# A build-time instruction order planned with other durations and a list of kept rank changes

## The chip, the cores and the metric

The kernel runs on one core of one Trainium2 chip. The metric is the device time of one execution in microseconds (us), lower is better. A program is compared with the one before it on the same chip, and the times shown are single executions and their median.

## The reference

Attention over 4 batches, 8 heads, 768 positions and 64 values for each head; three of the heads see every earlier position, five see only four sink positions and a window of 64. The 3072 x 512 result goes through a two-branch layer. In short:

```
scores = q @ k.T / 8;   scores[mask == 0] = -1e9
x = softmax(scores) @ v                          # per batch and head, joined to 3072 x 512
h1, h2 = x @ w1, x @ w2                          # 512 -> 1024
out = maximum(h1, h2) @ w_out                    # 1024 -> 512
```

## The kernel before

The heads are taken in pairs, four pairs to a batch: one pair of two full heads (FF), one of a full and a windowed head (FS), two of windowed heads (SS). So there are 16 pairs, called n0 to n15; n0 to n3 are batch 0, n4 to n7 batch 1, and so on. For a pair the work runs through these operations, whose function names are used below:

- `load_qk`, `load_v`: DMAs issued by SyncE (SP), all in one queue, in the order of the code; `cast_qk` and `cast_v` make bf16 of them, mostly on GpSimd (POOL).
- `turn` and `unturn` transpose q and k through TensorE (PE) for n0 to n7; `turn_squares` does it on VectorE (DVE) for n8 to n15.
- `mix_k` writes `kx`, the keys in the order that windowed heads want, with two copies, on DVE or POOL; `mix_v` writes `vx` on POOL.
- `scores` (PE, line 480) writes one PSUM tile `ps`; `exp` (ScalarE, ACT, line 497) makes `at` of it; `mask` (DVE, line 519) multiplies a 0/1 table into it, for n4 to n15 only (n0 to n3 have a bias matmul, line 453).
- `weighted` (PE, line 541) multiplies `at` with v, once for each score tile and each half of the positions; `normalise` (DVE, lines 556 and 558: one reciprocal, two products) divides and writes x.

When a batch has its x: `turn_x` (PE, line 574) and `take_x` transpose it, for each half; `up` (PE, line 590) multiplies with w1 - w2, eight column blocks fc0 to fc7 for each half tg0 and tg1; `relu` (ACT or DVE) evicts them to `g`; `down` (PE, line 617) makes one block of 128 rows, i0 to i5, in three parts of four matmuls (maximum(h1, h2) is relu(h1 - h2) + h2, so a product of w2 and w_out, `product`, line 690, is prepared and added); `take_out` evicts it and `store` writes it out. `subtract` (line 721, DVE or POOL) makes w1 - w2, `cast_w2` bf16 of w2, `turn_w2` its transpose.

All these are recorded as operations with a cost in microseconds for each engine that may do them. The class `Order` then plans them at build time: `Order.run` steps through modelled time, gives each engine the ready operation of lowest `rank` (the pair's number for most), takes PE's work from seven lists in the priority TX (turn_x), W (weighted), S (scores), TQ (turn), F (up, down), P (product), D (filler), picks one of four PSUM banks for each PE output, and emits the operations in the order found. On the chip each engine runs its instructions strictly in that order and waits by semaphores. So a cost never enters the program as time; it only decides which engine gets an operation and in which order each engine's instructions stand. A helper, `copy`, records most copies and casts, so they all have line 314 (ACT) or 316 (DVE and POOL).

Of the kernel before, what the change touches and what calls it, by code (L numbers as in the profile page):

```python
# [2 lines left out]

# [12 lines left out]
ACT = mybir.ActivationFunctionType  # L16
# [52 lines left out]
WARM = 60  # L69


class Op:


# [9 lines left out]
class Order:  # L84
# [5 lines left out]

    def __init__(self, banks):
        self.ops, self.lists, self.banks = [], {}, banks
        self.users, self.bank, self.queue = [None] * banks, None, None
        self.warm = 0.0

    def op(self, engine, cost, emit, deps=(), **more):
        o = Op(engine, cost, emit, deps, **more)
# [17 lines left out]
        o.behind, self.queue = self.queue, o  # L115
        return o

    def run(self, names, together=(), spare=(), until=0.0, begin=None):
        free = dict.fromkeys(("PE", "SP", "DMA", "ACT", "DVE", "POOL"), 0.0)
        free.update(begin or {})  # L120
        waiting, pending = [], []
        at = {n: 0 for n in names}
        for k, o in enumerate(self.ops):
            o.number = k
            o.left = sum(d.end is None for d in o.deps) + (o.behind is not None)
            for d in o.deps:
                d.users.append(o)
            if o.behind is not None:
                o.behind.followers.append(o)

        def arm(o, t):
            o.ready = max([t] + [d.end + d.tail for d in o.deps])
            if o.engine != "PE":
                heapq.heappush(waiting, (o.ready, o.number, o))

        def release(users, t):
            for u in users:
                u.left -= 1
                if u.left == 0:
                    arm(u, t)  # L140

        def finish(o, end):
            o.end = end
            release(o.users, 0.0)

        def free_bank():

            able = [
                (0.0 if u is None else u.end + u.tail, k)
                for k, u in enumerate(self.users) if u is None or u.end is not None  # L150
            ]
            return min(able) if able else None

        def when(o):

            if o.left:
                return None
            if o.bank:
                found = free_bank()
                return None if found is None else max(o.ready, found[0])  # L160
            return o.ready

        def pick():

            soon = None
            for n in names:
                mine = self.lists.get(n, ())[at[n]:at[n] + 2]
                w = when(mine[0]) if mine else None
                if w is None:
                    continue  # L170
                if n in spare and (t > until or soon and soon[1] < t + mine[0].cost["PE"]):
                    continue
                if n in together and len(mine) > 1 and not mine[0].single:
                    w2 = when(mine[1])
                    if w2 is not None and w2 < w + 2.0:
                        w = max(w, w2)
                if w <= t:
                    return n, w
                if soon is None or w < soon[1]:
                    soon = n, w  # L180
            return soon

        t = 0.0
        for o in self.ops:
            if not o.left:
                arm(o, 0.0)
        while True:
            while waiting and waiting[0][0] <= t:
                pending.append(heapq.heappop(waiting)[2])
            times = [waiting[0][0]] if waiting else []  # L190
            done = False
            for e in ("ACT", "DVE", "POOL", "SP"):
                able = [o for o in pending if e in o.cost or (o.engine == "DMA" and o.by == e)]
                if not able:
                    continue
                if free[e] > t:
                    times.append(free[e])
                    continue
                for o in sorted(able, key=lambda o: (o.rank, o.ready, o.number)):
                    if o.engine == "DMA":  # L200
                        free[e] = t + o.issue
                        start = max(free[e], free["DMA"])
                        free["DMA"] = start + o.cost["DMA"]
                        end = free["DMA"] + 1.6
                    else:
                        end = t + o.cost[e]
                        if any(max(free[x], t) + c < end for x, c in o.cost.items() if x != e):
                            continue
                        free[e] = end
                    pending.remove(o)  # L210
                    o.emit(e)
                    release(o.followers, t)
                    finish(o, end)
                    done = True
                    break
            if free["PE"] <= t:
                best = pick()
                if best and best[1] <= t:
                    n = best[0]
                    now = t  # L220
                    for k in range(2 if n in together and not self.lists[n][at[n]].single else 1):
                        mine = self.lists[n][at[n]:at[n] + 1]
                        w = when(mine[0]) if mine else None
                        if w is None or w > now + 0.3:
                            break
                        o = mine[0]
                        at[n] += 1
                        if o.bank:
                            self.bank = free_bank()[1]
                            self.users[self.bank] = o.bank  # L230
                        o.emit("PE")
                        now += o.cost["PE"] * (2 if now < self.warm else 1)
                        finish(o, now)
                    free["PE"] = now
                    done = True
                elif best:
                    times.append(best[1])
            else:
                times.append(free["PE"])
            if done:  # L240
                continue
            later = [x for x in times if x > t]
            if not later:
                break
            t = min(later)
        for n in spare:
            for o in self.lists.get(n, ())[at[n]:]:
                o.end = t
        left = sum(o.end is None for o in self.ops)
        assert not left, f"{left} operations were not reached"  # L250
        return t


def tile_paired_heads(tc, q, k, v, w1, w2, w2f, wo, out, tab, heads):
# [490 lines left out]
    def prepare_w12(half, rank):  # L745
        for two in range(2):
            if half:
                loaded = load(1.6, load_w2(half, two))
                prepare_w2(half, two, loaded, rank)
            else:  # L750
                loaded = w2_left[two]
            old, frees = take("qn")
            o = load(1.6, load_w1(half, two), old)
            for c in range(2):
                subs[half, two, c] = op(
                    None, {"DVE": 0.68, "POOL": 1.45}, subtract(half, two, c), [o, loaded], rank=rank
                )
                frees.append(subs[half, two, c])

# [4 lines left out]
    def prepare_qk(n):  # L764
# [22 lines left out]
            bfrees.append(un)  # L787
            ready.append(un)
        if "S" in SLOTS[n % HP]:
            cost = {"DVE": 0.8 if n < HP else 0.5, "POOL": 1.1}  # L790
            ready.append(op(None, cost, mix_k(n), [*ready], rank=n))
        k_ready[n] = ready

    def prepare_v(n):
        old, frees = take("vn")
        mine = [load(1.05, load_v(n, hh), [*old, sorted_], issue=0.5) for hh in range(2)]
        done_with["v", n] = take("v")
        cast = op("POOL", 0.88, cast_v(n), [*mine, *done_with["v", n][0]], rank=n)
        frees.append(cast)
        v_ready[n] = [cast]  # L800
        if "S" in SLOTS[n % HP]:
            cost = 0.5 if SLOTS[n % HP] == "FS" else 0.75
            v_ready[n] += [op("POOL", cost, mix_v(n, lower), [cast], rank=n) for lower in (True, False)]

    frees_ps = []
# [1 line left out]
    def attend(n):  # L807
        biased = n < HP
        for t in tiles_of[n]:
# [3 lines left out]
            if biased:  # L813
# [5 lines left out]
            e = op("ACT", 0.2 + sum(w) / 1240, exp(n, t), [s, *old], rank=n)  # L819
            frees_ps.append(e)  # L820
            mask_ops[n, t] = [e] if biased else [
                op("DVE", 0.13 + part[1] * part[2] / 1700, mask(n, t, *part), [e], rank=n)
                for part in mask_products(n, t)
            ] or [e]
            done_with["qk", n][1].append(s)
# [1 line left out]
        for half in range(2):  # L827
            mine = [t for t in tiles_of[n] if used(n, t, half)]
            if (p, half) == (0, 0):
                done_with["x", b] = take("x")  # L830
            norm = op("DVE", 1.0, normalise(n, half), [*done_with["x", b][0]], rank=n)
            for t in mine:
                w = pe(
                    "W", len(used(n, t, half)) * 0.031 + 0.03,
# [87 lines left out]
    for _ in range(WARM):  # L922
        pe("D", 0.43, warm, bank=order.given(0.0))

    order.warm = 8.4
    order.run(
        ("TX", "W", "S", "TQ", "F", "P", "D"), together=("S",), spare=("D",), until=20.0,
        begin={"DMA": 5.8, "SP": 4.6, "DVE": 5.4, "ACT": 4.8, "POOL": 5.0, "PE": 4.7},
# [536 lines left out]
```

## Time and profile before

| what | value |
| --- | --- |
| median of 3 runs | 190.68 us (189.26 to 191.23) |
| the profiled execution | 190.68 us, span of its instructions 188.6 us |
| TensorE busy | 173.3 us, 92% of the span |
| VectorE, ScalarE, GpSimd busy | 106.5, 113.7 and 61.5 us |
| mean granted TensorE clock | 0.997 |

The span runs from the first to the last instruction; some 2.1 us of the time lie outside it. PE, DVE, ACT, POOL and SP are the engines; a group `out<-in xcount` is named by the line that issued it and by the program's tiles.

### The profile page before, as it was taken

How to read it: one execution, taken by the hardware profiler on the slowest of the kernel's cores; microseconds unless marked ns; L12 is line 12 of the kernel's file. 1: busy time of each engine (PE TensorE's matmuls, PEld its weight loads, DVE VectorE, ACT ScalarE, POOL GpSimd, SP SyncE). 2: the span in 40 equal slices, each digit the busy share in tenths (PEclk: the TensorE clock that was granted, in tenths of full speed). 3: DMA queues.
4: the chain of work that ended last, by engine and by line, in shares of the span. 5: the costliest groups of instructions: out<-in, count | busy, mean ns of one | idle time of the engine just before them, and what ended most of it. 6: DMA issues, size and time to landing. Idle time of an engine off the chain costs nothing.

```text
span 188.6 us, 4670 instructions
## 1 busy us (share of the span) xinstructions
PE 173.3 (92%) x1706; PEld 101.4 (54%) x1706; DVE 106.5 (56%) x249; ACT 113.7 (60%) x167; POOL 61.5 (33%) x82
## 2 busy tenths in 40 slices
PE   0699997999999999999999998899999999999990
PEld 0456654666566556655655465445564545545560
DVE  4547869861599799989998779863740000000000
ACT  3079786778779687747964869275732714625420
POOL 0405496405787345263751526342000000000000
PEclk9999999999999999999999999999999999999998
DMA  5899999899997999999999999833002112012022
GB/s 178 271 303 315 213 287 366 275 299 320 298 286 125 152 153 152 184 169 207 154 200 157 185 191 189 220 150 118 2 30 84 56 57 89 23 59 111 0 107 75
DMA packets 86914, 32.11 MB, mean 170 GB/s; under 512 B 76387, under 2 KB 80739, under 8 KB 86883
## 3 DMA queue, kind: packets, MB, share of 16 engines
q1 hardware_dynamic: 86594, 31.34, 71.3%
q10 hardware_dynamic: 288, 0.39, 0.7%
q8 instruction: 15, 0.25, 0.6%
q14 instruction: 17, 0.13, 0.3%
HBM read 25.43 MB, written 6.29 MB: 168 GB/s over the span
## 4 chain that ended last, share of the span: by engine, by line
PE 74%; DVE 11%; DMA 5%; ACT 3%; issue 2%; POOL 2%; POOLq 1%; ACTq 0%; SPq 0%; DVEq 0%
PE pout L617 28%; PE ph L590 21%; PE po L541 7%; PE ps L480 6%; DVE at L519 5%; DMA w2f<-in_moe_w_dram 4%; PE pt L405 3%; PE po L690 3%; PE px L574 2%; DVE x L558 2%; ACT at L497 2%; PE pout L632 1%; DVE qk L418 1%; PE pw L676 1%; POOL w2b L316 1%
## 5 line engine op out<-in xcount | busy, mean ns | idle before, releaser
L497 ACT ACTIVATE at<-ps 128x1024 bf16<-128x1024 f32 (+3 forms) x68 | 59.4, 917 | 18.4 <-PE ps L480 17.9
L590 PE MATMUL ph<-xt,w 128*128 128x384 bf16 x256 | 44.8, 326 | 1.0 <-DVE g L603 0.8
L617 PE MATMUL pout<-wob,g 128*128 128x512 bf16 x184 | 45.1, 379 | 0.0
L316 POOL CAST qb<-qn 128x768 bf16<-128x768 f32 x26 | 22.8, 880 | 39.4 <-DMA qn<-in_k_dram 20.4
L590 PEld LDWEIGHTS <-w 128*128 128x128 bf16 x256 | 24.1, 98 | 17.3 <-issue 1.0
L601 ACT ACTIVATE g<-ph 128x384 bf16<-128x384 f32 x54 | 26.5, 492 | 9.0 <-PE ph L590 8.8
L519 DVE TENSOR_TENSOR at<-at,tab 128x1024 bf16<-128x1024 bf16 (+5 forms) x45 | 27.8, 644 | 4.6 <-ACT at L497 4.4
L314 ACT COPY ot<-pout 128x512 f32<-128x512 f32 (+1 forms) x22 | 12.7, 577 | 28.2 <-PE pout L617 26.2
L617 PEld LDWEIGHTS <-g 128*128 128x128 bf16 x184 | 16.8, 98 | 18.0
L316 DVE COPY ot<-pout 128x512 f32<-128x512 f32 (+1 forms) x3 | 1.8, 596 | 42.8 <-PE pout L632 42.3
L541 PEld LDWEIGHTS <-at 128*128 128x128 bf16 x472 | 19.8, 98 | 10.9 <-DVE at L519 2.9
L541 PE MATMUL po<-vb,at 128*128 128x65 bf16 x372 | 23.4, 194 | 2.1 <-DVE at L519 1.3
L558 DVE TENSOR_TENSOR x<-po,rez 128x192 f32 x64 | 22.9, 357 | 2.2
L617 PE MATMUL pout<-w2o,xt 128*128 128x512 bf16 x92 | 23.6, 379 | 0.0
L480 PE MATMUL ps<-qk 64*128 64x128 bf16 (+2 forms) x292 | 21.4, 234 | 0.0
L316 POOL CAST vb<-vn 128x768 bf16<-128x768 f32 x16 | 13.6, 850 | 17.1 <-DMA vn<-in_v_dram 14.5
L480 PEld LDWEIGHTS <-qk 64*128 64x128 bf16 x292 | 11.9, 94 | 11.0 <-issue 8.0
L316 POOL COPY vx<-vb 64x650 bf16<-64x650 bf16 (+1 forms) x24 | 17.1, 714 | 1.4
L418 DVE STREAM_TRANSPOSE qk<-qb 128x768 bf16<-128x768 bf16 x16 | 15.4, 965 | 0.0
L617 PEld LDWEIGHTS <-xt 128*128 128x128 bf16 x92 | 8.3, 98 | 8.5 <-issue 0.2
L541 PE MATMUL po<-vx,at 128*128 128x65 bf16 x100 | 10.8, 194 | 0.0
L480 PE MATMUL ps<-qk,kx 64*128 64x128 bf16 x100 | 9.7, 216 | 0.0
(57 smaller groups left out, 139.3 us busy)
## 6 DMA issues: line engine op xcount, KB each, us to landing
vn<-in_v_dram SPq DMA_DIRECT2D x32, 192.0 KB, 4.3
out_dram<-ot SPq DMA_DIRECT2D x23, 256.0 KB, 3.1
qn<-in_q_dram SPq DMA_DIRECT2D x16, 192.0 KB, 4.1
qn<-in_k_dram SPq DMA_DIRECT2D x16, 192.0 KB, 3.9
qn<-in_q_dram SPq DMA_DIRECT2D x32, 96.0 KB, 4.1
qn<-in_k_dram SPq DMA_DIRECT2D x32, 96.0 KB, 3.4
w2f<-in_moe_w_dram SPq DMA_DIRECT2D x4, 512.0 KB, 6.9
w1f<-in_moe_w_dram SPq DMA_DIRECT2D x4, 512.0 KB, 5.9
```

The source lines that it names most:

```text
L314: nc.scalar.copy(out=out, in_=in_)
L316: eng[e].tensor_copy(out=out, in_=in_)
L405: nc.tensor.transpose(pt[:, i:i + 128], T["qb", n][:, t, i:i + 128], ident)
L418: nc.vector.transpose(T["qk", n][:, t], T["qb", n][:, t])
L480: nc.tensor.matmul(ps[:, bank, e * 128:(e + m) * 128], lhsT=lhsT, rhs=qk[rows, 0, i * 128:(i + m) * 128], start=bank not in begun, stop=Tr ...
L497: nc.scalar.activation(out=at[:, 0:len(w), 0:w[0]], in_=T["ps", n, t][:, 0:len(w), 0:w[0]], func=ACT.Exp, scale=scale,)
L519: eng[e].tensor_tensor(out=at, in0=at, in1=tbl, op=ALU.mult)
L541: nc.tensor.matmul(po[:, hh, b[-1] - 3 * half, :], lhsT=at[:, bank, e * 128:(e + 1) * 128], rhs=rhs, start=first and (bank, hh, e, b) == m ...
L558: nc.vector.tensor_tensor(out=T["x", b][:, 3 * half:3 * half + 3, bass.ds(heads[2 * p + hh], 1), :], in0=po[:, hh, :, 0:D].unsqueeze(2), i ...
L590: nc.tensor.matmul(ph, lhsT=w12[:, kc, fc * 128:(fc + 1) * 128], rhs=xts[b % len(xts)][:, 3 * tg:3 * tg + 3, kc, :], start=(kc == 0), stop ...
L601: nc.scalar.activation(out=g[:, fc, :], in_=ph, func=ACT.Relu)
L617: nc.tensor.matmul(pout, lhsT=lhsT, rhs=rhs, start=(e == 0), stop=(e == len(steps) - 1))
```

## The change

The diff does three things. It gives other costs to some operations: a `subtract` 0.85 us on DVE and 1.3 on POOL, `mix_k` 0.6 on DVE from n4 on, `mix_v` 0.52 and 0.82, a `mask` 0.27 us plus its elements over 1850, a `normalise` 0.97. It splits `run` into `plan`, which finds the order, and `run`, which emits it; banks and ends are now kept in `plan`. And it adds `vary`: for each of 17 kept seeds a random generator picks 1 to 20 operations that are not PE's and adds a normal deviate of 2 to their `shift`, or sets it back to zero; engines now choose by `rank + shift`. The work itself, its shapes and its tiles are the same.

```
+SEEDS = (200006, 200015, 200048, ..., 201428)
...
+    def vary(self, seeds):
+        self.link()
+        movable = [o for o in self.ops if o.engine != "PE"]
+        for seed in seeds:
+            rng = random.Random(seed)
+            for o in rng.sample(movable, rng.choice((1, 2, 4, 8, 20))):
+                o.shift = o.shift + rng.gauss(0, 2.0) if rng.random() < 0.8 else 0.0
+
+    def run(self, *args, **more):
+        _, steps = self.plan(*args, **more)
+        for o, e, self.bank in steps:
+            o.emit(e)
...
-                for o in sorted(able, key=lambda o: (o.rank, o.ready, o.number)):
+                for o in sorted(able, key=lambda o: (o.rank + o.shift, o.ready, o.number)):
...
-                    None, {"DVE": 0.68, "POOL": 1.45}, subtract(half, two, c), [o, loaded], rank=rank
+                    None, {"DVE": 0.85, "POOL": 1.3}, subtract(half, two, c), [o, loaded], rank=rank
...
-            cost = {"DVE": 0.8 if n < HP else 0.5, "POOL": 1.1}
+            cost = {"DVE": 0.8 if n < HP else 0.6, "POOL": 1.1}
             ready.append(op(None, cost, mix_k(n), [*ready], rank=n))
...
-            cost = 0.5 if SLOTS[n % HP] == "FS" else 0.75
+            cost = 0.52 if SLOTS[n % HP] == "FS" else 0.82
...
-                op("DVE", 0.13 + part[1] * part[2] / 1700, mask(n, t, *part), [e], rank=n)
+                op("DVE", 0.27 + part[1] * part[2] / 1850, mask(n, t, *part), [e], rank=n)
...
-            norm = op("DVE", 1.0, normalise(n, half), [*done_with["x", b][0]], rank=n)
+            norm = op("DVE", 0.97, normalise(n, half), [*done_with["x", b][0]], rank=n)
...
     order.warm = 8.4
+    order.vary(SEEDS)
```

More of the change, by code (lines that the diff above doesn't have):

```diff
@@ L1 @@
 import heapq
+import random
 from contextlib import ExitStack
@@ L69 @@
 WARM = 60
+SEEDS = (
+    200006, 200015, 200048, 200090, 200092, 200121, 200145, 200150, 200168, 200200, 200225, 200453,
+    200472, 200557, 200589, 200748, 201428,
+)
 class Op:
@@ L92, in __init__ @@
         self.ops, self.lists, self.banks = [], {}, banks
-        self.users, self.bank, self.queue = [None] * banks, None, None
-        self.warm = 0.0
+        self.bank, self.queue = None, None
+        self.warm, self.linked = 0.0, False
     def op(self, engine, cost, emit, deps=(), **more):
@@ L116, in load, with link @@
         return o
[L118 to L122, printed above, removed]
+    def link(self):
         for k, o in enumerate(self.ops):
-            o.number = k
-            o.left = sum(d.end is None for d in o.deps) + (o.behind is not None)
+            o.number, o.shift = k, 0.0
             for d in o.deps:
@@ L129, in run, with plan @@
                 o.behind.followers.append(o)
+        self.linked = True
+    def vary(self, seeds):
[9 more added lines that the diff above has]
+            o.emit(e)
+    def plan(self, names, together=(), spare=(), until=0.0, begin=None):
+        if not self.linked:
+            self.link()
+        free = dict.fromkeys(("PE", "SP", "DMA", "ACT", "DVE", "POOL"), 0.0)
+        free.update(begin or {})
+        waiting, pending, steps = [], [], []
+        at = {n: 0 for n in names}
+        users = [None] * self.banks
+        for o in self.ops:
+            o.end, o.ready = None, 0.0
+        for o in self.ops:
+            o.left = sum(d.end is None for d in o.deps) + (o.behind is not None)
         def arm(o, t):
@@ L149, in free_bank @@
                 (0.0 if u is None else u.end + u.tail, k)
-                for k, u in enumerate(self.users) if u is None or u.end is not None
+                for k, u in enumerate(users) if u is None or u.end is not None
             ]
@@ L210, in run @@
                     pending.remove(o)
-                    o.emit(e)
+                    steps.append((o, e, None))
                     release(o.followers, t)
@@ L227, in run @@
                         at[n] += 1
+                        bank = None
                         if o.bank:
-                            self.bank = free_bank()[1]
-                            self.users[self.bank] = o.bank
-                        o.emit("PE")
+                            bank = free_bank()[1]
+                            users[bank] = o.bank
+                        steps.append((o, "PE", bank))
                         now += o.cost["PE"] * (2 if now < self.warm else 1)
@@ L245, in run @@
             t = min(later)
[L246 to L249, printed above, removed]
+        spared = {id(o) for n in spare for o in self.lists.get(n, ())[at[n]:]}
+        left = sum(o.end is None and id(o) not in spared for o in self.ops)
         assert not left, f"{left} operations were not reached"
-        return t
+        return max(o.end for o in self.ops if o.end is not None), steps
 def tile_paired_heads(tc, q, k, v, w1, w2, w2f, wo, out, tab, heads):
```

## The prediction

> **What bounds the kernel now.** I read the slices of the page first, then the busy time by stretches, then who TensorE waited for, then the single rows around those waits.
>
> ```profile
> PE   0699997999999999999999998899999999999990
> DVE  4547869861599799989998779863740000000000
> ```
> ```profile
> 80.00:100.00 20.00, 19.65 (x226) 11.44 (x225) 18.90 (x42) 13.89 (x21) 11.10 (x12) 1.00 1.05 181
> 100.00:120.00 20.00, 18.34 (x211) 11.35 (x210) 17.23 (x40) 13.88 (x19) 8.65 (x11) 1.00 1.10 179
> 140.00:184.30 44.30, 44.30 (x244) 23.40 (x240) 1.11 (x2) 18.40 (x36) 0.00 (x0) 1.00 0.18 66
> sum 149.30, PE 146.98 PEld 84.92 DVE 83.72 ACT 91.41 POOL 45.50; mean PE 21.00 PEld 12.13 DVE 11.96 ACT 13.06 POOL 6.50
> ```
>
> In each stretch the columns are its length, then busy time of PE, weight loads, DVE, ACT and POOL. The sum covers 35.0 to 184.3 us: PE is idle for 149.30 - 146.98 = 2.3 us of it, 1.7 of them from 100 to 120. From 140 on it never stops. The granted clock is 1.00 throughout. So PE bounds the kernel; the change leaves every matmul in the program, only in another order, and what it can win is PE's waiting. DVE, at 18.9 and 17.2 of 20 us, is nearly as full in the middle, and it is what PE waits for:
>
> ```profile
> PE po L541 <- DVE at L519: 1.3, 4, 0.4
> PE ph L590 <- DVE g L603: 0.8, 1, 0.8
> ```
> ```profile
> 51.28 0.42 PE L541 MATMUL po<-vb,at 128*128 128x65 bf16 x8 [0.17 <-DVE at L519]
> ...
> 99.00 0.19 PE L541 MATMUL po<-vx,at 128*128 128x65 bf16 x1
> 99.55 0.20 PE L541 MATMUL po<-vb,at 128*128 128x65 bf16 x1 [0.35 <-DVE at L519]
> ...
> 107.40 0.42 PE L541 MATMUL po<-vb,at 128*128 128x65 bf16 x8 [0.33 <-DVE at L519]
> ...
> 117.04 0.27 PE L541 MATMUL po<-vb,at 128*128 128x65 bf16 x3 [0.43 <-DVE at L519]
> ...
> 118.37 0.81 PE L590 MATMUL ph<-xt,w 128*128 128x384 bf16 x4 [0.81 <-DVE g L603]
> ```
>
> The masks of n11, n12 and n13 come late, and once the eviction of an `up` (`relu` of n13's stretch, queued on DVE behind four late masks and a transpose). The bracket understates a wait: 99.00 to 99.55 is 0.55 us where the narrow matmuls otherwise follow at 0.03 or 0.04, so 0.51 was lost, of which 0.35 shows as idle and 0.16 is covered by the last matmul still in flight. Those four stops are 1.92 us in brackets, 2.56 with 0.16 each. The other 2.32 - 1.92 = 0.4 us of idle lies in six small ones (at 51.3, 68.6, 77.2, 78.3, 108.8, 124.9), with the cover 1.36. Together 3.9 us from 35 on. Five of the ten follow a group of scores, and there a change of matrix shape costs something anyway:
>
> ```profile
> 67.82 0.19 PE L541 MATMUL po<-vx,at 128*128 128x65 bf16 x1
> 67.94 0.23 PE L480 MATMUL ps<-qk 64*128 64x128 bf16 x2
> ```
>
> 0.12 between the starts, 0.09 more than a narrow step. Less 5 x 0.09, the stops that an order can remove are **3.5 us**, 1.8% of the time.
>
> **Why the masks were late.** The DVE rows beside POOL's:
>
> ```profile
> 93.26 0.54 DVE L519 TENSOR_TENSOR at<-at,tab 128x768 bf16<-128x768 bf16 x1
> 97.08 1.31 DVE L519 TENSOR_TENSOR at<-at,tab 128x1024 bf16<-128x1024 bf16 x1
> 98.32 1.17 DVE L519 TENSOR_TENSOR at<-at,tab 128x768 bf16<-128x768 bf16 x1
> 132.37 0.68 DVE L519 TENSOR_TENSOR at<-at,tab 128x1024 bf16<-128x1024 bf16 x1
> ```
> ```profile
> 96.59 1.26 POOL L316 CAST qb<-qn 128x768 bf16<-128x768 f32 x1 [2.12 <-DMA qn<-in_k_dram]
> 98.08 1.01 POOL L316 CAST vb<-vn 128x768 bf16<-128x768 f32 x1 [0.23 <-DMA vn<-in_v_dram]
> ```
>
> A 128x1024 mask takes 0.68 alone and 1.31 when it starts inside a POOL cast; 768 wide it is 0.54 and 1.17. Both late ones end 0.4 to 0.5 us after the cast (97.85, 99.09). So 0.63 us is what such a meeting costs. The Trainium skill, page "SBUF — State Buffer", section "Who interferes with whom", says that a DVE instruction with two SBUF inputs contends with a GpSimd instruction that reads SBUF, and that the later one fully blocks; the trace agrees. The planner has no such term, before or after.
>
> **The change part by part.** I compared the built instruction order of both programs engine by engine.
>
> *Up to 32 us* PE, ACT and SP are unchanged. *32 to 35 us*: the chain is
>
> ```profile
> 23.35 8.29 DMA w2f<-in_moe_w_dram
> 31.70 1.05 POOL w2b L316
> 32.79 0.63 PE pw L676 x8
> 33.45 1.01 ACT w2t L314
> 34.46 0.50 ACT xt L314
> 35.00 9.98 PE ph L590 x60
> ```
> ```profile
> 31.40 0.18 DVE L556 RECIPROCAL rez<-po 128x6 f32<-128x6 f32 x1
> 32.29 0.18 DVE L556 RECIPROCAL rez<-po 128x6 f32<-128x6 f32 x1
> L316 DVE CAST wob<-wof 128x1024 bf16<-128x1024 f32 x4 | 2.7, 687 | 1.8 <-DMA wof<-in_moe_w_out_dram 1.8
> ```
>
> `cast_w2` goes from POOL (1.05) to DVE (0.69), so `turn_w2` starts 0.35 earlier. But it stands ahead of both `normalise` of n3 (0.89 each by the two starts), which before ran from 31.40 while the weights were still landing. Now: cast to 32.4, normalise to 33.3 and 34.2, then `take_x` 0.69, so the first `up` at about 34.9. Gain 0.1 at most, loss 0.9 if all of the shifted normalise showed; I take 0.
>
> *The subtractions.*
>
> ```profile
> SPq L703 <- DVE w L721: 5.1, 2, 3.6
> L721 DVE TENSOR_TENSOR w<-w1f,w2f 128x512 bf16<-128x512 f32 x6 | 5.1, 875 | 1.0 <-DMA w1f<-in_moe_w_dram 1.0
> L721 POOL TENSOR_TENSOR w<-w1f,w2f 128x512 bf16<-128x512 f32 x2 | 2.5, 1270 | 0.4 <-DMA w1f<-in_moe_w_dram 0.3
> ```
>
> SP waits 5.1 us for two of them before it issues the w_out loads, and every load of n4 and later is queued behind. DVE does three instead of six, POOL five instead of two, and DVE gets the two casts. POOL's last one can end at about 37 to 38 us against 37.98 for DVE's now, so the loads move 0 to 1 us earlier. No stop listed above names a DMA; worth nothing directly, I take 0.
>
> *`mix_k` of n9, n11 and n14 to POOL.*
>
> ```profile
> 92.93 0.40 DVE L316 COPY kx<-qk 128x320 bf16<-128x320 bf16 x2
> 126.79 1.09 POOL L316 COPY kx<-qk 128x320 bf16<-128x320 bf16 x2 [2.45 <-DVE qk L418]
> ```
>
> DVE is relieved of 3 x 0.40 = 1.2 us, not 3 x 0.6 as the planner reckons; POOL gets 3 x 1.09. Relus and evictions change places both ways (batch 1: three relus on DVE instead of two in tg0, two instead of four in tg1; some take_x and take_out to DVE), so I count on a relief of 0.5 us rather than 1.2 between 64 and 120. What stands behind: on POOL `mix_k` waits for the transpose on DVE, and the next casts wait behind it.
>
> *PE's order from 59 us on.* This is the term that decides. Unit prices:
>
> ```profile
> 130.54 0.55 PE ps L480 x16
> ...
> 139.50 0.67 PE px L574 x12
> ...
> 145.35 5.20 PE ph L590 x32
> 150.56 7.77 PE pout L617 x36
> ```
>
> Two score tiles cost 0.55, an `up` 5.20 / 8 = 0.65, a part of a `down` 7.77 / 9 = 0.86. At each big stop I add up what stands between scores and the product that waited:
> - n11: before, one part (0.86) from the last scores to the first `weighted`. After, six parts and the scores of n12, 6 x 0.86 + 0.55 = 5.7 us. The three masks with both meetings (0.68 + 1.31 + 1.17 = 3.2) fit and leave 2.5 us for the exp ahead of them.
> - n12: before, two parts, a product and a pair of scores from the first scores to the stop, some 2.6 us. After, n11's products, five parts, most of turn_x and two pairs of scores, over 5 x 0.86 + 2 x 0.55 = 5.4 us.
> - n13: before, three ups and 0.55, 2.5 us. After, fc5 to fc7, a part and 0.55, 3.4 us; and fc7 now writes a bank that ACT freed long ago, so the 0.98 us stop on `relu` fc6 has no cause left.
> - The small ones at 68.6 and 124.9 get one part (0.86) more ahead; 51.3 keeps its order and its loss, 0.17 + 0.16 - 0.09 = 0.24.
>
> Going down the new lists with these prices, I find four new close places, with 0.1 to 0.3 us to spare: `weighted` n8 t2 behind its mask, `turn_x` b2 (3,4), which needs the bank of (0,1), `up` b1 tg1 fc2, which needs the bank of n12's second normalise, and n13 t1. If one meeting of 0.63 falls ahead of each, each loses up to 0.5; if none does, nothing. I take half, 4 x 0.25 = 1.0, and 0.24 at 51.3.
>
> So 3.5 - 1.0 - 0.24 = 2.26 us fewer stops; groups of scores fall from 42 to 41, each with a change in and out: -0.1 to -0.2, I take 0.1; the opening 0. Sum -2.3 or -2.4; against the profiled execution, 190.68, which is also the median: **188.4 us**. Bounds: everything removed 3.5 + 0.2 + 0.1 gives 186.9; full price at the close places (2.0), the stop at 51.3 and the opening's 0.9 gives 190.68 - (3.5 - 2.0 - 0.24 - 0.9) = 190.3.
>
> **The rivals.**
> 1. *The meetings simply fall elsewhere.* By the same sign, a mask well over its time alone, a mask of n6 to n14 met a POOL instruction some eight times. The new order knows nothing of it and POOL is busier by 3.3 us in that stretch; with nine meetings, five of them at places with under 0.5 us to spare, stops are 5 x 0.6 = 3.0, and the time is 190.68 - 0.5 = 190.2. For it: PE waits for masks, and masks are late by this. Against: n11 and n12 have several us to spare. By the Trainium skill, page "SBUF — State Buffer", section "Who interferes with whom", each of the six new `kx` copies could stop a mask for up to its own 0.55, 3.3 us in all; that would end at the same place or a little higher.
> 2. *`mix_k` on POOL becomes the wait (slower).* Scores of n9, n11 and n15 need it about 0.9, 1.1 and 0.5 us before PE gets there. Its place on POOL is fixed, ahead of the `vx` copies and later casts, and it starts only when DVE's transpose is done. It decides once DVE runs some 2 us behind my count: then PE waits 1.1 + 0.9 + 1.5 = 3.5 us there, and 0.9 at n14's first mask, which has 1.1 to spare. 190.68 - 2.4 + 4.4 = 192.7. For it: DVE is 86 to 95% busy there. Against: before, DVE had idle moments in every 20 us, and it is relieved.
> 3. *No effect.* The order of PE does change from 59 us on, so this can only be if the stops are chance; the three runs spread by 2 us. It gives the same time as the first rival.
>
> **How the numbers follow.** One per cent, 1.9 us, is about what a measurement here tells from no change; faster means under 188.8, slower over 192.6 us. Forecast 0.62, of which 0.45 ends under 188.8 and 0.17 between it and 190; rivals 1 and 3 0.23, all within 1%; rival 2 0.15, which I count as slower throughout. Faster 0.45, same 0.40, slower 0.15. Low end 187.2, short of the full 186.9, because 51.3 keeps its wait; high end 190.9, which takes in the first rival with 0.7 us over for places that I did not see, and leaves out the second.
>
> **What would show it.** Right: PE's idle from 35 us on falls from 2.3 to about 1 us; no wait of an `up` for DVE's relu; `weighted` of n11 and n12 without a bracket; attention done (last `turn_x`) some us before 139.5. Wrong: brackets naming kx or qk ahead of scores (rival 2), or masks of 1.1 us or more right ahead of new brackets (rival 1); the first `up` later than 35.5 (the opening).

## The result, and the profile after

The changed kernel takes 188.68 us, the median of 21 runs (187.33 to 192.70); the kernel before takes 189.98 in the 21 runs beside them (188.77 to 192.14). The ratio is 0.9941, interval 0.9914 to 0.9969: 1.1 us faster, by 0.6 to 1.6; it leaves out, here and below, runs more than 1.5% above the fastest of their kernel, while the medians count them and differ by 1.3. The profiled execution took 188.4 us, its span 186.6; before it was 190.68 and 188.6.

The slices of the page, TensorE and VectorE:

```profile
PE   0689996999999999999999999999999999999990
DVE  4537869932588789999799997889540000000000
```

The two eights at the slices 25 and 26 of before (113 to 123 us) are gone; the seventh slice, the opening, went from seven tenths to six. The same stretches as before (length; busy PE, weight loads, DVE, ACT, POOL; clock; DMA), from 35 us to the last matmul:

```profile
80.00:100.00 20.00, 19.90 (x231) 11.69 (x231) 18.39 (x43) 12.91 (x19) 10.74 (x16) 1.00 1.05 171
100.00:120.00 20.00, 19.66 (x218) 11.79 (x215) 18.34 (x39) 13.45 (x19) 8.96 (x13) 1.00 1.10 165
sum 147.30, PE 144.95 PEld 84.16 DVE 84.05 ACT 89.85 POOL 48.33; mean PE 20.71 PEld 12.02 DVE 12.01 ACT 12.84 POOL 6.90
```

From 100 to 120 us the idle time fell from 1.7 to 0.3 us. The sum would say 147.30 - 144.95 = 2.35 us of idle, as much as before, and that is misleading: this trace holds 1684 of the 1706 matmuls, and a missing record reads as idle time. So I go by the waits, and by the starts of neighbouring rows:

```profile
PE po L572 <- DVE at L550: 0.4, 2, 0.2
PE po L572 <- DVE ot L347: 0.4, 1, 0.4
PE pout L648 <- issue: 0.3, 2, 0.2
```
```profile
50.58 0.38 PE L511 MATMUL ps<-qk 64*128 64x384 bf16 x4
51.10 0.27 PE L572 MATMUL po<-vb,at 128*128 128x65 bf16 x3
...
60.49 0.27 PE L572 MATMUL po<-vb,at 128*128 128x65 bf16 x3 [0.20 <-DVE at L550]
...
78.15 0.64 PE L572 MATMUL po<-vb,at 128*128 128x65 bf16 x15 [0.38 <-DVE ot L347]
...
117.24 0.20 PE L572 MATMUL po<-vb,at 128*128 128x65 bf16 x1 [0.23 <-DVE at L550]
```

`issue` I put down to missing records. The rest, with the stop at 51.10 that has no bracket, counted as in the prediction (bracket and cover, less 0.09 where the shape of the matrix changes), is 0.21 + 0.37 + 0.45 + 0.40 = 1.4 us of stops, against 3.5 before. No `up` waits for DVE, and `weighted` of n11 and n12 have no bracket.

The opening:

```profile
28.90 7.60 POOL L752 TENSOR_TENSOR w<-w1f,w2f 128x512 bf16<-128x512 f32 x5
```
```profile
30.64 1.75 DVE L347 CAST w2b<-w2f 128x1024 bf16<-128x1024 f32 x1
```
```profile
32.45 0.62 PE L707 MATMUL pw<-tab,w2b 128*128 128x128 bf16 x8 [0.66 <-DVE w2b L347]
33.34 1.73 PE L605 MATMUL px<-tab,x 128*128 128x128 bf16 x24 [0.27 <-DVE x L589]
34.92 2.27 PE L621 MATMUL ph<-xt,w 128*128 128x384 bf16 x13
```

The first `up` starts at 34.92, before at 35.00. In this execution the opening gave nothing and took nothing.

### The profile page after: what moved, and what is told of

Same layout as the page of the kernel before. It is cut to its first block, busy times and chain, and to the rows that moved or that the text cites. A ratio compares the mean times of both kernels' runs of the same rounds, so it can differ in the third digit from the quotient of the medians.

```text
span 186.6 us, 4650 instructions
## 1 busy us (share of the span) xinstructions
PE 169.9 (91%) x1684; PEld 100.1 (54%) x1706; DVE 107.9 (58%) x244; ACT 112.0 (60%) x165; POOL 65.6 (35%) x89
## 4 chain that ended last, share of the span: by engine, by line
PE 78%; DVE 8%; ACT 4%; issue 3%; DMA 3%; SPq 2%; ACTq 0%; DVEq 0%
PE pout L648 31%; PE ph L621 22%; PE po L572 8%; PE ps L511 7%; ACT at L528 4%; DVE at L550 4%; PE px L605 3%; PE pt L436 2%; DMA qn<-in_q_dram 2%; PE po L721 2%; PE pout L663 1%; SPq L374 1%; PE ps L484 1%; DVE x L589 1%; DMA raw<-in_is_retrieval_dram 1%
## 5 line engine op out<-in xcount | busy, mean ns | idle before, releaser
L621 PE MATMUL ph<-xt,w 128*128 128x384 bf16 x256 | 44.1, 327 | 0.0
L648 PE MATMUL pout<-wob,g 128*128 128x512 bf16 x179 | 43.4, 379 | 0.5 <-issue 0.3
L632 ACT ACTIVATE g<-ph 128x384 bf16<-128x384 f32 x56 | 27.5, 491 | 9.7 <-PE ph L621 9.6
L347 POOL CAST qb<-qn 128x768 bf16<-128x768 f32 x26 | 22.1, 852 | 28.3 <-DMA qn<-in_k_dram 15.6
L550 DVE TENSOR_TENSOR at<-at,tab 128x1024 bf16<-128x1024 bf16 (+5 forms) x45 | 28.6, 665 | 1.8 <-ACT at L528 1.6
L347 DVE COPY ot<-pout 128x512 f32<-128x512 f32 (+1 forms) x6 | 3.8, 632 | 43.3 <-PE pout L663 42.3
L345 ACT COPY ot<-pout 128x512 f32<-128x512 f32 (+1 forms) x19 | 10.9, 575 | 25.5 <-PE pout L648 23.5
L572 PE MATMUL po<-vb,at 128*128 128x65 bf16 x372 | 22.0, 195 | 1.6 <-ACT at L528 0.5
L572 PEld LDWEIGHTS <-at 128*128 128x128 bf16 x472 | 18.6, 98 | 8.9 <-DVE at L550 1.3
L345 ACT COPY qk<-pt 128x768 bf16<-128x768 bf16 x11 | 8.9, 806 | 1.4 <-PE pt L436 1.4
```

Source lines behind the costliest of these rows:

```text
L345: nc.scalar.copy(out=out, in_=in_)
L347: eng[e].tensor_copy(out=out, in_=in_)
L550: eng[e].tensor_tensor(out=at, in0=at, in1=tbl, op=ALU.mult)
L572: nc.tensor.matmul(po[:, hh, b[-1] - 3 * half, :], lhsT=at[:, bank, e * 128:(e + 1) * 128], rhs=rhs, start=first and (bank, hh, e, b) == m ...
L621: nc.tensor.matmul(ph, lhsT=w12[:, kc, fc * 128:(fc + 1) * 128], rhs=xts[b % len(xts)][:, 3 * tg:3 * tg + 3, kc, :], start=(kc == 0), stop ...
L632: nc.scalar.activation(out=g[:, fc, :], in_=ph, func=ACT.Relu)
```

## The experiments

**Which stretch holds the gain.** Two kernels join the two orders at the first `up` of the second half of w12 (`up` b0 tg1 fc6, about 44 us). The planner's run is replaced by a written list of steps (operation, engine, bank):

```
-    order.run(("TX", "W", "S", "TQ", "F", "P", "D"), ...)
+    for step in STEPS.split():     # h1: changed order up to the join, old order behind it; h2: the reverse
+        ...
+        order.ops[number].emit(engine)
```

Theory A is the prediction's: the gain is TensorE's order from 59 us on. R1 is that it comes from the opening and the earlier loads.

h1_opening_new: 

> Opening of the new order (everything planned ahead of the up b0 tg1 fc6, so subtractions, cast_w2 and n3's normalise as in the changed kernel), all later operations in the old order. Theory A (the gain is PE's order from 59 us on): as before, 190.0 us within 0.6, PE's stops from 50 us on about 3.5 us with the late masks of n11, n12 and n13 back. Rival R1 (the gain comes from the opening: loads of n4 and later issued up to 1 us earlier): 188.7 us, stops under 2 us.

h2_rest_new: 

> Opening of the old order, all operations from the up b0 tg1 fc6 on in the new order and banks. Theory A: the whole gain, 188.6 us within 0.6, stops of PE from 50 us on about 1.4 us. Rival R1: as before, 190.0 us.

Measured: with the new opening alone 190.44 us against 190.13 of before in the same session (ratio 1.0004, 0.9952 to 1.0056); with the new order of the rest alone 188.82 (0.9941, 0.9889 to 0.9992), the whole change's ratio. Theory A holds and R1 falls. Of the first one's expectation the time came and the stops did not: its profile has no wait of 0.2 us or more at the masks of n11, n12 and n13 (see "Do the stops come back"). TensorE's waits in the second one from 35 to 140 us are one line:

```profile
PE po L589 <- DVE at L567: 0.6, 1, 0.6
```

**Which part of the change.** The diff has two parts, the durations and the rank changes of the search.

```
c_costs_only                     s_seeds_only
-SEEDS = (200006, ...)           -{"DVE": 0.85, "POOL": 1.3}         +{"DVE": 0.68, "POOL": 1.45}
+SEEDS = ()                      -0.27 + part[1] * part[2] / 1850    +0.13 + part[1] * part[2] / 1700
                                 ...  (mix_k, mix_v and normalise as before, too)
```

c_costs_only: 

> The new costs without the seeds: the planner's own order. It puts mix_k of n11, n13, n14 and n15 on POOL. Theory A expects a time by its stops alone: if the better mask costs are what matters, 188.7 to 189.2 us with stops of 1.5 to 2 us; if the kept rank changes are, 189.5 to 190.5 with 2.5 to 3.5 us.

s_seeds_only: 

> The old costs with the 17 seeds, whose shifts were kept for other costs. mix_k of five pairs goes to POOL. Rank changes that help only together with the costs they were kept for: no gain, 189.5 to 191 us. If rank changes help by themselves: 188.7 us.

Measured: the durations alone 188.84 us (0.9962, 0.9919 to 1.0004); the seeds on the old durations 193.44 (1.0192, 1.0121 to 1.0264). So the new durations alone get within 0.2 us of the whole change, which these runs can't separate from it (nor, by a hair, from no change). The seeds are worth nothing on the old durations: they were kept for another set, and here they cost 3.3 us against the 190.13 of the session, more than either expectation had. Where is only in part known: the one profile is the longest of the six runs (196.03 us). Three others, at a clock of 0.997 or more, still took 192.2 to 192.6 us. In the profile x comes late in the opening, TensorE stops 1.36 us and the clock falls (below):

```profile
36.51 1.46 PE L605 MATMUL px<-tab,x 128*128 128x128 bf16 x12 [1.36 <-DVE x L589]
37.77 1.49 PE L621 MATMUL ph<-xt,w 128*128 128x384 bf16 x4
```
```profile
35.00:42.00 7.00, 5.64 (x29) 3.29 (x27) 5.75 (x12) 3.15 (x6) 0.02 (x1) 0.51 0.75 259
```

**Are late masks the cause?** Both orders without the 45 multiplications by the masks of n4 to n15; their outputs lack those masks.

```
 def mask(n, t, bank, banks, cols, at_table):
...
-            eng[e].tensor_tensor(out=at, in0=at, in1=tbl, op=ALU.mult)
```

nb_no_masks_before: 

> The order of the kernel before with the 45 multiplications of the causal and the window mask of n4 to n15 on DVE left out (their weighted follow the exponential at once; the output lacks these masks). Theory A, 'the old order loses its time to masks that come late': the net stops from 35 us on, 3.5 us, shrink to under 1 us, 187.5 us. Rival 'the order of TensorE's groups itself costs it': 189 or more, and 1 us above the changed order without masks.

na_no_masks_after: 

> The changed order with the same 45 multiplications left out. Theory A: net stops of 1.0 to 1.4 us shrink to some 0.5, 187.9 us, within 0.5 us of the order of before without masks. Rival 'the order of TensorE's groups itself': as far below the order of before without masks as the kernels with masks are apart, 1.1 us.

Measured: 187.85 (0.9895, 0.9857 to 0.9934) and 187.77 us (0.9897, 0.9856 to 0.9939). The old order gains 2.2 us, the new one about 0.9 against its median of another session, and they end together; with six runs each, 1 us between them is at the edge of what the intervals exclude. But in its profile the old order's stops without masks did not shrink to under 1 us, as theory A had it:

```profile
PE ph L636 <- DVE g L649: 0.7, 1, 0.7
PE ph L636 <- ACT ot L360: 0.6, 1, 0.6
PE pt L451 <- ACT g L647: 0.5, 1, 0.5
```
```profile
114.85 0.98 DVE L464 STREAM_TRANSPOSE qk<-qb 128x768 bf16<-128x768 bf16 x1 [1.61 <-POOL qb L362]
115.75 0.52 DVE L649 TENSOR_SCALAR g<-ph 128x384 bf16<-128x384 f32 x1
```

The first of the three is the stop at 118.37 of the profile before. With no mask on DVE its `relu` is still late, now because the transpose ahead of it waits 1.61 us for POOL's cast. What the old order lacked there was time between that `relu` and the `up` that needs its bank; the masks were one of two things to use it up. And behind the opening the two do not tie: from the start of the first `up` to the end of the span the two profiles without masks take 186.6 - 34.23 = 152.4 and 186.1 - 35.03 = 151.1 us. So that the masks make the whole difference between the orders is not shown.

**Do the stops come back at the same places?** Both kernels again, each with its own order written out as a list.

b2_before_again: 

> The kernel before with its order written out as a list, step by step the same: a second profiled execution of the same work. Theory 'a late mask is a matter of the order': stops from 35 us on at the places of the first profile (99.5, 107.4, 117.0, 118.4), 3.5 us in all. Rival 'the order leaves little slack, and each execution pays for it somewhere': about the same sum, 2.9 to 3.7 us, at other places. Time 190.0.

a2_after_again: 

> The changed kernel with its order written out, step by step the same: a second profiled execution. By the first theory the stops of 51.1, 60.5, 78.1 and 117.2 come back; by the rival 0.8 to 1.9 us of stops lie anywhere, of those places foreseen (masks of n8 t2 and n13 t1, the transposition of x, the third up of the second batch) one or two at most. Time 188.7.

Measured: 189.99 us (10 runs; 0.9965, 0.9912 to 1.0017) and 188.59 (4 runs; 0.9852, 0.9766 to 0.9938), beside 190.57 of before; the profiled ones took 188.38 and 188.9. Their waits from 35 to 140 us, of before's order:

```profile
PE ph L638 <- DVE g L651: 0.7, 1, 0.7
PE pout L665 <- issue: 0.2, 1, 0.2
```

and of the changed order:

```profile
PE po L589 <- DVE at L567: 0.5, 1, 0.5
PE pout L665 <- issue: 0.3, 2, 0.2
```

```profile
115.84 0.81 PE L638 MATMUL ph<-xt,w 128*128 128x384 bf16 x4 [0.71 <-DVE g L651]
```
```profile
61.96 0.60 PE L589 MATMUL po<-vb,at 128*128 128x65 bf16 x5 [0.49 <-DVE at L567]
```

Of the four big stops of before, one came back, the `relu` at 115.84; the three late masks at 99, 107 and 117 did not. The sum was 1.5 us in this execution, not 2.9 to 3.7. Of the changed order's stops only the one near 61 (n5) came back.

Three kept profiles can be set beside these. h1 has the old order behind 44 us; its waits, and after them a row each of h2 and of w_fill (below), which have the new one there:

```profile
PE po L589 <- DVE at L567: 1.2, 3, 0.6
PE ph L638 <- DVE g L651: 0.2, 1, 0.2
```
```profile
60.94 0.27 PE L589 MATMUL po<-vb,at 128*128 128x65 bf16 x3 [0.63 <-DVE at L567]
```
```profile
62.47 0.27 PE L590 MATMUL po<-vb,at 128*128 128x65 bf16 x3 [0.63 <-DVE at L568]
```

The mask stops of h1 lie at 60.6 and 61.5 (n5) and at 75.3 us. So there are both kinds. The three late masks of n11 to n13 are in one of three profiles of the old order; its stop on `relu` is in all three (0.81, 0.71, 0.24), and without masks, too. The stop at n5 is in all four profiles of the new order (0.20, 0.49, 0.63, 0.63) and in h1. By the waits that are listed from 35 us on, without `issue`, the old order lost 2.1, 0.7 and 1.4 us, the new one 0.8, 0.5, 0.6 and 0.8.

A figure that takes in small stops as well is the time from the first `up` to the end of the span. The profiles that have one of the two orders step by step behind 44 us (without h3 and h4 below, in which work on w2 moves behind the first `up`):

| order behind 44 us | profiles: span less start of first `up`, us | mean |
|---|---|---|
| before | 188.6 - 35.00 = 153.6; 186.3 - 34.49 = 151.8; h1: 189.5 - 35.58 = 153.9 | 153.1 |
| changed | 186.6 - 34.92 = 151.7; 187.1 - 35.78 = 151.3; h2: 185.7 - 35.13 = 150.6; w_fill (below): 188.7 - 36.54 = 152.2 | 151.4 |

h1's figure holds 0.8 us of a halved clock and that of 187.1 half a microsecond (last section); without these the means are 152.8 and 151.3. By the means the order behind 44 us is worth about 1.5 us, but on three and four executions whose ranges overlap; two of the old one lie 1.8 us apart.

**The second rival, `mix_k` on POOL.**

```
 (mix_k n9), (mix_k n11), (mix_k n14), (mix_k n15), at their places in the changed order:
-    POOL
+    DVE
```

k_mix_dve: 

> The changed order with the mixed keys kx of n9, n11, n14 and n15 copied by DVE in place of POOL, at the same places in the order (0.25 us for each of the eight copies in place of 0.45). If putting them on POOL cost something, as the second rival of the prediction has it, this is faster: 188.2 or less. If their time on POOL is free and DVE is the engine that is short, each of the four puts 0.5 us ahead of a mask and the time rises by up to 1 us where a mask is late by it: 188.7 to 189.5. I take the latter.

Measured: 188.91 us (12 runs; 0.9921, 0.9887 to 0.9956), beside 188.59 and 188.68 of the changed order. (The ratio owes something to a session in which before took 190.57; the old order written out took 189.99 there.) Putting the copies on POOL cost nothing that shows; taking them back doesn't help. The copies on POOL, in the changed kernel, take 0.45 us each, two to a `mix_k`, where the prediction reckoned 0.55 from the row of two:

```profile
L347 POOL COPY kx<-qk x8: 448/454/456, 79.6 to 125.3; 128x320 bf16<-128x320 bf16 x6, 64x320 bf16<-64x320 bf16 x2
```

**A better opening?** The kernel with the durations alone starts its first `up` at 33.58, since it leaves the cast of w2 on POOL and turns w2's second half later. Its opening, joined to the changed order of the rest; and the same with both transpositions of w2 behind the last `up` of that stretch:

```
 h4 against h3, around the end of the first ups:
-    turn_w2 (1, 0); take_w2 (1, 0) on ACT; turn n4 t0; relu tg1 fc5 on ACT; up tg1 fc6; ...; turn_w2 (1, 1); take_w2 on DVE
+    turn n4 t0; relu tg1 fc5 on ACT; up tg1 fc6; ...; turn_w2 (1, 0); take_w2 on DVE; turn_w2 (1, 1); take_w2 on ACT
```

h3_costs_opening: 

> The opening of the kernel planned with the new durations but without the seeds (no cast of the matrix w2 on DVE, first up at 33.58 us there, the transposition of w2's second half after the ups), then the changed kernel's order of everything else. Theory 'each stretch for itself': the opening is worth 34.92 - 33.58 = 1.34 us less 0.62 us of the transposition that comes later, 0.7 us, and the rest keeps its stops of 0.8 to 1.4 us: 187.9 us, ratio to before 0.989. Rival 'the loads of n4 set the pace behind the opening': TensorE gets to n4's and n5's transpositions 0.7 us earlier than the queries and keys do, waits for POOL's qb at 43.7 and 58.2 (0.39 and 0.26 us in the kernel without seeds), and the time stays at 188.7.

h4_opening_fixed: 

> The joined order with the opening of the kernel without seeds again, but with the transpositions of w2's second half side by side behind the last up of that stretch and their evictions on DVE and behind the unturn of n4 on ACT, so that no relu stands behind them (that took the 1.32 us at 46.4). If that stop was the whole loss of the joined kernel: 189.1 - 1.3 = 187.8 us, faster than the changed kernel. Rival 'POOL's casts of n4's queries and keys set the pace there': a stop of 0.4 to 0.7 us between 43 and 50 us, 188.4.

Measured: 189.10 us (0.9966, 0.9931 to 1.0001) and 188.79 (0.9895, 0.9834 to 0.9957; 6 runs). Both missed their theories' 187.9 and 187.8. The first one's profile has its longest stop where a `relu` stands on ACT behind the eviction of w2:

```profile
44.93 1.01 ACT L362 COPY w2t<-pw 128x1024 bf16<-128x1024 bf16 x1 [0.61 <-PE pw L724]
45.84 0.50 ACT L649 ACTIVATE g<-ph 128x384 bf16<-128x384 f32 x1
```
```profile
46.39 1.46 PE L638 MATMUL ph<-xt,w 128*128 128x384 bf16 x8 [1.16 <-ACT g L649]
```

In the second that stop is down to 0.4 us (0.24 in the bracket), and it is no faster than the changed order of the same session. Their first `up` started at 35.18 and 35.24 in the profiled executions and not at 33.6 (the second under a halved clock, below), so the early opening itself did not come back. No version with the whole work that I ran is faster than the changed kernel by more than the spread of the runs.

**Filling the opening's idle time.**

```
+    warm x2        # ahead of weighted n3 t2 half1
+    warm x3        # ahead of turn_w2 half1 two0
+    warm x1        # ahead of turn_x b0 (0, 1)
```

w_fill: 

> The changed kernel with six matmuls of the kind that warms TensorE at the start (128x512, no use of their result) put into the idle time of the opening: two ahead of the last weighted of n3, three ahead of the transposition of w2, one ahead of that of x. They lengthen nothing if the idle time there is as in the profile (0.52, 0.66 and 0.27 us; six take 1.3 us at full clock). Theory 'half-clock stretches begin in the idle opening and make up much of the spread': with TensorE's busy share from 30.7 us up from .58 to about .9, no run shows a granted clock below 0.995, the runs spread over less than 1 us and the median falls to 188.0. Rival 'the spread has another source': clocks and median as in the changed kernel, 188.7 (189.0 where the fillers delay the ups by 0.3).

Measured: 188.57 us (13 runs; 0.9946, 0.9915 to 0.9977). Of the time, the rival holds: the median is the changed kernel's, and the runs spread over 2.6 us, not less than 1. Of the clock, the theory holds in part: five of the 13 runs lie below its 0.995, but none below 0.992 (see the last section).

## Why the prediction was right, and where not

*The time.* 188.4 was forecast, 188.68 measured, inside the range. But the step from the stops to the time was made against one execution of 190.68, "which is also the median" of the three runs then shown. The median of 21 is 189.98, so the gain is 1.1 us by the ratio and 1.3 by the medians, and not the 2.3 of the sum. That the time came out so near is in part luck: the starting point was 0.7 us above the later median, and the gain 1 us too large. The sum agrees with its own execution: stops of 3.5 fell to 1.4, 2.1 us fewer. The term that failed is the size of what can be removed: 3.5 us was what one long execution of the old order showed, and the second one showed 1.5.

*TensorE's order decides.* Right as to the stretch, and shown: the new order of the rest alone gives the whole ratio, the new opening alone none. (The rest includes the order of the other engines, which was not tested apart from TensorE's.)

*The cause of the stops.* Half right. Masks that meet a POOL instruction make stops; in the profile of the changed kernel the two mask stops left, at n5 and n13, follow such masks as well. The one ahead of 60.49 ran beside POOL's copies of vx (59.43 to 61.03), and a mask of its shape without POOL took 0.41 us in h1:

```profile
59.50 0.94 DVE L550 TENSOR_TENSOR at<-at,tab 128x512 bf16<-128x512 bf16 x1
```
```profile
62.29 0.41 DVE L567 TENSOR_TENSOR at<-at,tab 128x512 bf16<-128x512 bf16 x1
```

But "the masks of n11, n12 and n13 come late" was read as a property of the order, and two further profiles of it show it to be a matter of the moment. Of the four big stops only the one on `relu` belongs to the old order (0.81 at 118.37, 0.71 at 115.84, 0.24 in h1, 0.7 without masks). The prediction gave its removal a reason that fits: fc7 writes a bank that ACT freed long ago, and no profile of the new order has the stop. Which stops make up the rest of the 1.1 us stays open.

*The meetings stay.* The masks, shape by shape, in before and after:

```profile
L519 DVE TENSOR_TENSOR at<-at,tab 128x1024 bf16<-128x1024 bf16 x12 | 9.6, 814 | 2.1 <-ACT at L497 2.1
L519 DVE TENSOR_TENSOR at<-at,tab 128x768 bf16<-128x768 bf16 x9 | 7.2, 804 | 0.4 <-ACT at L497 0.3
```
```profile
L550 DVE TENSOR_TENSOR at<-at,tab 128x1024 bf16<-128x1024 bf16 x12 | 10.5, 904 | 0.0
L550 DVE TENSOR_TENSOR at<-at,tab 128x768 bf16<-128x768 bf16 x9 | 7.3, 812 | 0.1
```

The mean mask is as slow as before or slower (904 and 812 ns, against 0.68 and 0.54 us alone). So these masks did not get faster. (How many meet POOL differs from execution to execution: the 768 wide ones took 622 ns in the mean in the old order's second profile.) What changed by the program is how much of TensorE's work lies between a mask and its product: the prediction's count of parts between scores and `weighted` at n11, n12 and n13. That this slack makes the gain is argued and not shown, since two of the three profiles of the old order stop there for no 0.2 us either. Rival 1, which had the meetings fall on close places again, has the time wrong (190.2) and the mechanism right for n5 and n13.

*The four close places, 4 x 0.25.* Of them only n13 t1 stopped in the first profile (0.40), and none in the second. Near n8 there was a stop (78.15, 0.45), not for its mask but for a bank that `take_out` held. One at n5 (60.49, and 61.96 in the second) was not foreseen: there the scores of n5 had moved ahead of its first `weighted`, and I followed the order only where before had shown a stop. That stop came in all four profiles of the new order that stand in the table. The sum, 1.24 forecast and 1.4 measured, agrees more by luck than by its parts.

*The signs.* The last transposition of x began at 137.11 us instead of 139.34, as foreseen; but it did so at 136.77 in the old order's second profile, so this is no sign of the new order.

*The opening, taken as 0.* Right in the sum (34.92, forecast 34.9), wrong in a term: the cast of w2 on DVE was put at 0.69 us and took 1.75 inside POOL's five subtractions. In w_fill it began while POOL waited (31.8 to 32.6 us):

```profile
32.23 0.68 DVE L365 CAST w2b<-w2f 128x1024 bf16<-128x1024 f32 x1
```

By the Trainium skill, page "SBUF — State Buffer", section "Who interferes with whom", a cast on DVE is among the operations that can, under conditions on their operands, enter a mode with two ports and then contend with GpSimd, and whichever starts first blocks the other. The rows agree: 1.75 us beside the subtractions, 0.68 without. The prediction had weighed that section for masks only, not for this cast. The loss was paid by luck: the cast could start at 30.64 us, since the weights landed some 1 us earlier in this execution than in before's, where POOL waited for them until 31.70.

*Rival 2.* No wait names kx ahead of scores in the changed kernel, and the copies back on DVE gain nothing. Waits for kx elsewhere are small: 0.2 us in the new order without masks, 0.3 in w_fill and in h3, and 0.7 in h1, where DVE made most of the copies.

*Rival 3, chance.* It has more to it than its share in the text: three of the four big stops of the first profile are chance, and in each order one other is not (the `relu`, and the mask of n5). The difference between the orders is not chance, by the intervals that lie below 1 (the change, h2, w_fill, k_mix_dve, the second writing of the changed order), while the old order written out lies at 0.9912 to 1.0017.

## What to carry to other kernels

A list of stops read from one execution tells which kind of wait costs time; which places will cost it in the next, it tells only in part. Take the gain against the median of many runs, and profile the same program several times before a stop is called the order's. Count the slack everywhere (how much of the bottleneck engine's work lies between a producer and its consumer), and not only where the first profile stopped: the new order's own stop lay elsewhere. In a planner, durations nearer to the means that a busy profile shows may act as margins: by the medians they brought nearly the whole gain here, though their interval reaches no change, while rank changes kept by a search are bound to the durations that they were found with, and cost 2% on others. When a stretch of one order is joined to another, look at each in-order queue at the seam: one eviction ahead of one `relu` stopped TensorE for 1.3 us.

## What the runs showed of the hardware that was not expected

TensorE's granted clock can halve for a stretch of 3.4 us right after the opening, where it has waited for x and w2 (33.5 to 36.9 us in the changed kernel's second execution; 35.2 to 42.0, twice as long, with the seeds alone). Two stretches of three profiles, the changed kernel, its second execution and the copies on DVE, and the first stretch of the filled opening. The columns are as above, the clock stands after POOL.

```profile
30.70:34.10 3.40, 1.96 (x34) 1.46 (x30) 3.26 (x9) 1.68 (x2) 3.26 (x3) 1.00 1.06 377
33.50:36.90 3.40, 3.36 (x37) 2.40 (x36) 3.37 (x6) 3.10 (x5) 3.00 (x3) 1.00 0.88 292
```
```profile
30.70:34.10 3.40, 1.84 (x28) 1.43 (x25) 3.26 (x8) 1.56 (x2) 2.96 (x3) 0.92 1.05 381
33.50:36.90 3.40, 3.40 (x28) 2.89 (x27) 2.82 (x6) 2.25 (x3) 3.06 (x3) 0.51 0.91 337
```
```profile
30.70:34.10 3.40, 1.69 (x27) 1.37 (x26) 3.23 (x8) 1.40 (x2) 3.03 (x3) 0.99 1.06 377
33.50:36.90 3.40, 3.40 (x29) 2.51 (x30) 3.01 (x6) 2.29 (x3) 2.92 (x3) 0.57 0.91 291
```
```profile
30.70:34.10 3.40, 3.19 (x35) 1.34 (x36) 3.30 (x8) 1.78 (x2) 2.56 (x3) 1.00 1.01 324
```

With 1.6 to 2.2 of the first 3.4 us busy the clock fell in some executions and not in others: of the profiles with 2.2 us or less, five of eight had the drop, and of the six with 2.6 or more none. The mean clock of the five was 0.977 to 0.991, that of the nine others 0.994 or more. Of the changed kernel's 21 runs 10 are at 0.991 or less; without the two over 192 us their median is 189.0, against 188.4 of the others. Of the 13 with the filled opening none is there. So the drop went away with 1.3 us of idle time filled with useless matmuls, but the median did not fall; what the fillers or something else gave back, no run shows. What decides between a drop and none at the same busy share, these runs don't tell.

The Trainium skill, page "TensorE: Matmul & The Clock Gate", section "HAM oscillation — how this bites in real kernels", gives as the rule that TensorE should have no idle gap longer than about 3.4 us. Here the clock fell after single gaps of 0.3 to 0.9 us in four profiles and of up to 1.7 in the fifth, 1.2 to 1.8 us of them within 3.4. The section "A second HAM failure mode: psum-queue depth-cycling" of the page says of a kernel that cycles through PSUM banks that frequent short idling did it too; that fits, though the short waits here were for `at` of the exponential, w2 and x. The section "What's actually happening" has the window run freely, not from the kernel's start; that would make some executions of one kernel drop and others not, and no run here shows it.
